# Sliding-window attention and a GeGLU block on one core: the first batch's opening run loaded in f32 by one queue, its row sums inverted on ScalarE, and two out tiles computed by halves

## The chip, the core and the metric

The kernel runs on one core of a Trainium2 chip. TensorE (PE in the profile) multiplies, VectorE (DVE) and ScalarE (ACT) work on its results, GpSimd (POOL) here clears memory and issues loads, SyncE (SP) issues transfers. All transfers share the core's 16 DMA engines. The metric is device time in microseconds of one execution; the kernel before took 346.55 us (median of three runs, 346.27 to 348.04).

## The reference

Attention with a window of 128 keys and a penalty that grows with distance, then a gated feed-forward block over all tokens. Inputs and the result are f32.

```python
# q, k, v: (8 batches, 8 heads, 576, 64)
scores = scale * np.matmul(q, k.transpose(0, 1, 3, 2))
rel = pos[:, None] - pos[None, :]
bias = slopes[:, None, None] * (-np.abs(rel))[None]
mask = (rel >= 0) & (rel < 128)
attn = softmax(np.where(mask, scores + bias, -1e9))
x = np.matmul(attn, v)                  # to (4608 tokens, 512)
g, val = x @ w_gate, x @ w_val          # 512 x 1536 each
out = (gelu(g) * val) @ w_out           # 1536 x 512
```

## The kernel before

A batch has 576 rows, a group of the feed-forward block 512 tokens, so that nine groups follow eight batches. The work of each engine stands in an order written out by hand (`manual_schedule`); what is emitted first for an engine is done first on it. PSUM has eight banks; `bank()` takes the one that came free longest ago. Attention of a batch is computed in between the out tiles of the group before it; only batch 0 has nothing ahead of it, and the change is there.

**Heads and pairs.** Two heads share 128 partitions: pair c holds heads 2c and 2c+1, and there are four pairs. Scores are computed with keys on the partitions, so that the probabilities `P` serve as the right operand for the values without a transpose; the sums over keys are matmuls with ones.

**Loading batch 0.** Its q and k come in two "runs" (`RUNS`): rows 0 to 383, three consecutive rows to a partition, and rows 384 to 575. Of the first run, heads 0 to 3 come as f32 by SP (q) and ScalarE (k), two heads a load, into `raw`, which borrows space of `wo`; `cast` makes bf16 of a pair (`pairs0`), and `first` transposes it, three matmuls for a pair, with `untangle` copying the result to `qT` or `kT`. Heads 4 to 7 come by POOL's queue, which casts on the way (`load_runs(0, 0, 4, 8)`, line 127), and `second` transposes them head by head (twelve matmuls a tensor). The second run also comes by POOL into `vb[1]`, is copied by VectorE to `pairs1` (line 728), and is transposed by `rest`. After these, POOL issues v of the batch (three tiles, then two), the gate and value weights in pieces of columns, batch 1's q and k, the last weights, both halves of w_out (line 774), and batch 1's v. A load on POOL's queue is issued only when the eighth one before it has landed.

**Scores of the first 384 rows.** `biases0` puts the distance penalty of a pair in two banks by a matmul with `slopes`, `scores0` adds the scores, and an exp on ScalarE of 128x512 a head writes `P` (line 193). Scores of the remaining rows come later (`scores0_rest`): they get their penalty by a multiplication with `emask` on VectorE (line 196). `emask` is made by `decays` on ScalarE, 192 columns a head, and its last columns by copies on VectorE (`masks_of_last_blocks`, line 672).

**Sums and values of the first 384 rows.** `sums4` collects the sums of all heads in 32-row parts of one bank with `ones8` (line 343), VectorE inverts them (line 348). `products_first` multiplies P with v in four banks, and ScalarE copies them to `recip` (line 490). `spread_first` spreads the inverses over 64 rows a head by sixteen f32 matmuls with `sel8` (line 357) and multiplies on VectorE into `xT` (line 518). For batches 1 and 2 the kernel has another way, in `values_and_sums`: sums in 64 rows a head with `ones64`, inverted on ScalarE as Exp(-Ln(x)) (lines 452 and 453), no spread. The last 192 rows of batch 0 have a third: `products_rest`, `inverse_rest` (reciprocals, line 509), `scale_rest`.

**Group 0.** `gate_val(g, f, lo, hi)` multiplies 128 columns of the gate and value weights with tokens lo to hi of xT; Gelu on ScalarE (line 545) and a product on VectorE (line 546) write `hT`. Block f=0 comes as two halves of 192 tokens, f=1 to 8 with 384 tokens, then f=0 to 8 with the other 128, then f=9 to 11 with all 512. Then come twelve matmuls for each of four out tiles (`out_part`, line 575, in quarters of three), with batch 1's scores, sums and values between; `todo[0]` holds the order. Functions of one table of ScalarE must be loaded before they are used; the first load in the head is for Exp, the second for Gelu.

**Two halves of a bank.** Where matmuls with key rows 0 to 63 and rows 64 to 127 add into one bank, `products` and `sums4` let a no-op of SP or VectorE stand between them (`relay`, line 318), which waits for the first half and releases the second.

Of the kernel before, what the change touches and what calls it, by code (L numbers as in the profile page):

```python
# [7 lines left out]
FP32 = mybir.dt.float32  # L8
# [13 lines left out]
COLUMNS0 = ((0, 192, 384), (None, None, 448, 640, 832))  # L22
# [5 lines left out]
def kernel(  # L28
# [32 lines left out]

    def bank():
        return psum.tile([128, 512], FP32, name="ps")
# [22 lines left out]
    sel0 = consts.tile([128, 8], FP32, name="sel0")  # L86
    sel8 = consts.tile([128, 4, 64], FP32, name="sel8")
# [147 lines left out]
    def scores0(cs, pss):  # L235
        for c, ps in zip(cs, pss):
            for n in range(3):
                for x in (0, 1):
                    q0 = 128 * n + 64 * x
                    w = min(192, 384 - q0)  # L240
                    for i in (0, 1):
                        score(0, c, i, 2 * n + x, q0, w,
                              ps[i][64 * x:64 * x + 64, 192 * n:192 * n + w], False)
        for c, ps in zip(cs, pss):
            for i in (0, 1):
                exp(prob(0)[:, c, i, 0:512], ps[i])


    def scores0_rest(cs, later):
        pss = []  # L250
        for c in cs:
            ps = [bank(), bank()]
            pss.append(ps)
            for n, skip, w, col in ((2, 64, 128, 0), (3, 0, 192, 128), (4, 0, 64, 320)):
                for x in (0, 1):
                    for i in (0, 1):
                        score(0, c, i, 2 * n + x, 128 * n + 64 * x + skip, w,
                              ps[i][64 * x:64 * x + 64, col:col + w])
        for c, ps in zip(cs, pss):
# [3 lines left out]
            later.append((dst, emask[:, 2 * c:2 * c + 2, 64:448]))  # L263
# [58 lines left out]
    def sums4(b, s, between=None, added=True):  # L322
        first, w = shape(b, s)
        ps = bank()
        mms = ([], [])
        for h in range(H):
            for x in (0, 1):
                t = first + w * x
                g, a = 2 * x + h // 4, 32 * (h % 4)
                if b and added:  # L330
                    mms[0].append((g, ones8[:, a:a + 32], T[:, h, t:t + w], 0, w))
                    continue
                for m, q0, q1, col in pieces(b, t, t + w):
                    half = slice(64 * (m % 2), 64 * (m % 2) + 64)
                    mms[m % 2].append((g, ones8[half, a:a + 32],
                                       Ps[b % 2][half, h, col:col + q1 - q0], q0 - t, q1 - t))
        for half in (0, 1):
            if half and mms[1]:
                by = relay(mm)
                if between:  # L340
                    between()
            for n, (g, lhsT, rhs, lo, hi) in enumerate(in_turn(mms[half]) if mms[half] else ()):
                mm = nc.tensor.matmul(  # L343
                    out=ps[32 * g:32 * g + 32, lo:hi], lhsT=lhsT, rhs=rhs,
                    start=half == 0 and n < 4, stop=True, skip_group_check=True)
                if half and n == 0:
                    depends(mm, by)
        nc.vector.reciprocal(row(b)[:, first:first + w], ps[:, 0:w])  # L348

    def spread4_banks(b, s):  # L350
        lo, w = shape(b, s)
        pss = [bank() for _ in range(4)]
        for n in (0, 1):

            rows = sel8[:, 2 * n:2 * n + 2, :].rearrange("p i m -> p (i m)")
            for g, ps in enumerate(pss):
                nc.tensor.matmul(  # L357
                    out=ps[:, w * n:w * n + w], lhsT=rows[32 * g:32 * g + 32, :],
                    rhs=row(b)[32 * g:32 * g + 32, lo:lo + w], start=True, stop=True,
                    tile_position=(32 * g, 0))  # L360
        return pss

    def spread4(b, s, copies):
        lo, w = shape(b, s)
        for g, ps in enumerate(spread4_banks(b, s)):
            c, x = 2 * (g % 2), g // 2
            copies[g](out=recip[b][:, c:c + 2, lo + w * x:lo + w * x + w],
                      in_=ps[:, 0:2 * w].rearrange("p (c x) -> p c x", c=2))
# [21 lines left out]
    def products(b, banks):  # L390
        pss = [bank() for _ in range(1 + max(u[0] for u in banks))]
        todo, mid = [], 0
        for x in (0, 1):
            at = 0
            for odd in (x, 1 - x):
                if odd != x:
                    mid = at = max(at, mid)
                wide, small = [], []
                for u, c, lo, hi, to in banks:
                    if u % 2 == odd:  # L400
                        (small if hi - lo == 64 else wide).extend(
                            (x, u, c, m, q0, q1, col, to, lo, hi)
                            for m, q0, q1, col in pieces(b, lo, hi) if m % 2 == x)

                ns, n = len(small), len(small) + len(wide)
                for k in range(n):
                    t = (small if (k + 1) * ns // n > k * ns // n else wide).pop(0)
                    todo.append((at, *t))
                    at += (t[5] - t[4]) * (1 if isinstance(t[2], int) else t[2].stop - t[2].start)
# [77 lines left out]
    def products_first(copies):  # L487
        n = PARTS[0][0][1]
        for c, ps in enumerate(products(0, [(c, c, 0, n, 0) for c in range(4)])):
            copies[c](out=recip[0][:, c, 0:n], in_=ps[:, 0:n])  # L490
# [22 lines left out]

    def spread_first():
        _, w = shape(0, 0)
        for g, ps in enumerate(spread4_banks(0, 0)):
            c, x = 2 * (g % 2), g // 2
            nc.vector.tensor_tensor(  # L518
                out=xT[:, c:c + 2, w * x:w * x + w], in0=recip[0][:, c:c + 2, w * x:w * x + w],
                in1=ps[:, 0:2 * w].rearrange("p (c x) -> p c x", c=2), op=ALU.mult)  # L520
# [67 lines left out]

    def out_last(g):
        for lo in (0, 256):  # L590
# [16 lines left out]
    raw = [wo[:, 3 + 3 * w:6 + 3 * w, :].rearrange("p a x -> p (a x)").bitcast(FP32)  # L607
           for w in (0, 1)]

    pairs0 = [t[0].rearrange("p j x -> p (j x)")[:, 0:768].rearrange(  # L610
        "p (x c y) -> p x c y", x=3, c=2) for t in (qs, ks)]
    pairs1 = wo[:, 9:12, :]
    for h in (0, 2):
        for w, src, queue in ((0, q, nc.sync), (1, k, nc.scalar)):
            queue.dma_start(
                out=raw[w].rearrange("p (h x) -> p h x", h=4)[:, h:h + 2, :],
# [4 lines left out]
    load_runs(0, 0, 4, 8)  # L621
# [10 lines left out]
    nc.gpsimd.memset(ones64, 1.0)  # L632
# [21 lines left out]
    def cast(w, c, copy):  # L654
        copy(out=pairs0[w][:, :, c, :].rearrange("p x (i d) -> p x i d", i=2),
             in_=raw[w].rearrange("p (c i x d) -> p c x i d", c=2, i=2, x=3)[:, c])

    made_slopes(0, 4)
    nc.vector.tensor_reduce(
        out=sel0, in_=ident.rearrange("p (g h r) -> p h g r", g=4, r=4)[:, :, :, 0],  # L660
        op=ALU.add, axis=mybir.AxisListType.X)

    load_w(512, 768)
    load_w(768, 1024)
    load_w(1024, 1280)
    for n in (0, 1):
        load_runs(1, n, 0, 8)
    load_w(1280, DFF)
# [15 lines left out]
    def rest(w, cs, copy):  # L684
        ps = bank().bitcast(BF16)
        p = 64 * w
        for n, c in enumerate(cs):
            for x in range(3):
                nc.tensor.transpose(
                    out=ps[:, 192 * n + 64 * x:192 * n + 64 * x + 64],  # L690
                    in_=pairs1[p:p + 64, x, 128 * c:128 * c + 128],
                    identity=ident[p:p + 64, p:p + 64])
        untangle(copy, 0, 1, w, cs[0], cs[-1] + 1, ps)

    def second(w, copies):
        ps = bank().bitcast(BF16)
        for c in (0, 1):
            transpose_runs(0, 0, w, 2 + c, ps[:, 384 * c:384 * c + 384])
        for c in (0, 1):
            untangle(copies[c], 0, 0, w, 2 + c, 3 + c, ps[:, 384 * c:384 * c + 384])  # L700

    held = [bank(), bank()]
    keep_busy(held[0], 10, 128)
    keep_busy(held[0], 44)
    decays(0, 2)
    cast(0, 0, dve)
    cast(1, 0, act)
    decays(2, 4)
# [5 lines left out]
    made_slopes(4, 8)  # L714
    ps0 = biases0((0,), 4)
    scores0((0,), ps0)
    held = [bank(), bank()]
    for w in (0, 1):
        first(w, 1, (dve, act)[w], held[w])
    second(0, (dve, dve))  # L720
    for t in kT + qT:
        nc.vector.memset(t[:, :, 576:640], 0.0)
    scores0((1,), biases0((1,)))
    second(1, (dve, dve))
    for c in (2, 3):
        scores0((c,), biases0((c,)))
    decays(5, 6)
    dve(out=pairs1.rearrange("p x (h d) -> p x h d", d=64),  # L728
        in_=vb[1].rearrange("p j x -> p (j x)")[:, 0:1536].rearrange(
            "p (h x d) -> p x h d", h=H, x=3))  # L730
    for cs in ((0, 1), (2, 3)):
        for w in (0, 1):
            rest(w, cs, dve)
    row(0)
    masks = []
# [5 lines left out]

    nc.scalar.copy(out=sel8, in_=sel0[:, 0:8:2].unsqueeze(2).to_broadcast((128, 4, 64)))
    sums4(0, 0, lambda: scores0_rest((0,), masks))
    products_first((act, act, act, act))
    masks_of_last_blocks(0, 4)
    for t in vb:
        nc.vector.memset(t[64:128, 4, :], 0.0)
    spread_first()
    decays(6, 8)
# [135 lines left out]
```

## Time and profile before

| what | us |
|---|---|
| median of three runs | 346.55 (346.27 to 348.04) |
| the profiled execution | 345.86 |
| its span, first to last instruction | 344.1 |
| PE busy | 333.4 (97%) |
| VectorE busy | 191.3 (56%) |
| ScalarE busy | 173.1 (50%) |
| first exp of scores starts | 6.74 |
| copy of the second run (line 728) starts | 11.04 |
| first gate matmul (line 539) starts | 18.29 |
| load of the Gelu table starts | 21.15 |
| gate of f=2 starts | 23.51 |
| first out tile (line 575) starts | 44.83 |

Times inside the execution count from the start of the span. A row of the profile names the line of the kernel, the engine, the operation, output and inputs, and the number of instructions; in square brackets stands the idle time of that engine just ahead of them, and what ended it. A matmul's end is modelled, so that the time from one start to the next says more about PE's pace than the length of one does. The granted clock of PE was 1.0 throughout.

### The profile page before, as it was taken

To read this page: it belongs to the slowest core of one execution; us is meant where nothing else is said; L and a number is where in the kernel's file an instruction comes from. 1 tells how busy PE (TensorE), PEld (TensorE's weight loads), DVE (VectorE), ACT (ScalarE), POOL (GpSimd) and SP (SyncE) were. 2 spreads that over 40 slices of the span, in tenths; PEclk is the share of its full clock that TensorE was granted. 3 is DMA by queue.
4 is the path that set the end of the run, shared out by engine and by line. 5 is a ranking of instruction groups with operands and counts; after the bars stand their busy time and mean duration, and the time that the engine had idled before them with its cause. 6 is when DMAs were issued, how large, how long until landed. Compare 5 with 4: busy or idle time off the path is not lost.

```text
span 344.1 us, 8080 instructions
## 1 busy us (share of the span) xinstructions
PE 333.4 (97%) x3299; PEld 171.0 (50%) x3338; DVE 191.3 (56%) x337; ACT 173.1 (50%) x334; POOL 107.6 (31%) x143
## 2 busy tenths in 40 slices
PE   8789999999999999999999999999999999999995
PEld 6566655444644454445444454445444544444443
DVE  6899564644589555944695369546774313303320
ACT  6674588537896338443753366344823133223322
POOL 9775763571193085008600680040000000000000
PEclk9999999999999999999999999999999999999999
DMA  9999999999699799989986999597115110020002
GB/s 171 171 196 190 206 168 120 146 170 186 133 142 175 149 155 183 200 156 111 183 176 130 113 181 183 94 141 102 63 34 107 61 65 0 0 93 30 0 32 91
DMA packets 149705, 43.09 MB, mean 125 GB/s; under 512 B 134532, under 2 KB 142628, under 8 KB 149668
## 3 DMA queue, kind: packets, MB, share of 16 engines
q0 software_dynamic: 108480, 18.49, 72.5%
q1 hardware_dynamic: 37744, 17.70, 22.1%
q10 hardware_dynamic: 3444, 6.38, 8.7%
q8 instruction: 26, 0.43, 0.5%
q14 instruction: 11, 0.09, 0.1%
HBM read 43.65 MB, written 9.53 MB: 155 GB/s over the span
## 4 chain that ended last, share of the span: by engine, by line
PE 91%; ACT 2%; DMA 2%; DVE 2%; issue 1%; POOL 1%; DVEq 0%; POOLq 0%; ACTq 0%
PE ps L539 53%; PE ps L575 27%; PE ps L425 5%; PE ps L188 2%; DMA vb<-in_k_dram 2%; PE ps L343 1%; ACT osb L580 1%; ACT P L193 1%; PE ps L593 1%; PE ps L144 1%; DVE xT L518 1%; DVE P L196 0%; ACT rb L452 0%; PE ps L357 0%; DVE wo L728 0%
## 5 line engine op out<-in xcount | busy, mean ns | idle before, releaser
L546 DVE TENSOR_TENSOR hT<-ps,gelu 128x512 bf16<-128x512 f32 (+3 forms) x118 | 74.3, 641 | 92.4 <-PE ps L539 80.3
L545 ACT ACTIVATE gelu<-ps 128x512 bf16<-128x512 f32 (+3 forms) x118 | 65.3, 561 | 103.3 <-PE ps L539 87.6
L539 PE MATMUL ps<-xT,wv 128*128 128x512 bf16 (+3 forms) x468 | 112.4, 361 | 0.4
L539 PE MATMUL ps<-xT,wg 128*128 128x512 bf16 (+3 forms) x457 | 111.2, 360 | 1.3 <-DVE xT L518 0.6
L575 PE MATMUL ps<-wo,hT 128*128 128x512 bf16 x402 | 94.4, 379 | 1.6 <-issue 0.6
L539 PEld LDWEIGHTS <-wv 128*128 128x128 bf16 x472 | 44.9, 98 | 48.8
L539 PEld LDWEIGHTS <-wg 128*128 128x128 bf16 x472 | 44.2, 98 | 48.7 <-issue 0.9
L193 ACT ACTIVATE P<-ps 128x384 bf16<-128x384 f32 (+2 forms) x128 | 56.1, 543 | 17.9 <-PE ps L188 17.7
L575 PEld LDWEIGHTS <-hT 128*128 128x128 bf16 x420 | 39.4, 98 | 46.7
L196 DVE TENSOR_TENSOR P<-P,emask 128x768 bf16<-128x768 bf16 (+1 forms) x60 | 34.5, 588 | 22.0 <-ACT P L193 21.1
L102 POOL DMA_DIRECT2D vb<-in_v_dram x40 | 33.8, 876 | 8.4 <-PE ps L188 2.2
L580 ACT COPY osb<-ps 128x512 f32<-128x512 f32 x29 | 17.4, 600 | 36.7 <-PE ps L575 36.5
L102 POOL DMA_DIRECT2D qs<-in_q_dram x30 | 25.2, 855 | 6.2 <-DMA wo<-in_moe_w_out_dram 4.4
L102 POOL DMA_DIRECT2D ks<-in_k_dram x30 | 25.4, 886 | 1.4 <-DMA qs<-in_q_dram 1.3
L836 POOL COPY mark<-hT 1x2 bf16<-1x2 bf16 x4 | 0.7, 176 | 78.6 <-DVE hT L546 78.6
L188 PE MATMUL ps<-qT,kT 64*64 64x192 bf16 (+2 forms) x656 | 19.3, 236 | 0.5 <-DVE kT L152 0.2
L188 PEld LDWEIGHTS <-kT 64*64 64x64 bf16 x656 | 13.0, 106 | 11.6 <-issue 8.1
L482 DVE TENSOR_TENSOR xT<-ps,rb 128x512 bf16<-128x512 f32 (+3 forms) x29 | 14.3, 564 | 6.4 <-PE ps L425 6.4
L425 PE MATMUL ps<-P,vb 64*64 64x192 bf16 (+2 forms) x736 | 17.5, 222 | 0.2
L425 PEld LDWEIGHTS <-vb 64*64 64x64 bf16 x736 | 14.6, 107 | 4.1 <-issue 2.7
L274 DVE TENSOR_TENSOR T<-P 64x1024 bf16<-64x1024 bf16 (+1 forms) x20 | 15.0, 751 | 0.4
L348 DVE RECIPROCAL r<-ps 128x128 f32<-128x128 f32 (+2 forms) x11 | 11.2, 1052 | 0.5 <-PE ps L343 0.5
(83 smaller groups left out, 156.5 us busy)
## 6 DMA issues: line engine op xcount, KB each, us to landing
out_dram<-osb SPq DMA_DIRECT2D x35, 256.0 KB
rb<-rd ACTq DMA_DIRECT2D x10, 576.0 KB
vb<-in_v_dram POOLq DMA_DIRECT2D x32, 128.0 KB, 6.4
qs<-in_q_dram POOLq DMA_DIRECT2D x24, 128.0 KB, 5.3
ks<-in_k_dram POOLq DMA_DIRECT2D x24, 128.0 KB, 6.3
wo<-in_moe_w_out_dram POOLq DMA_DIRECT2D x2, 768.0 KB, 14.7
wg<-in_moe_w_gate_dram POOLq DMA_DIRECT2D x5, 256.0 KB, 8.2
wv<-in_moe_w_val_dram POOLq DMA_DIRECT2D x5, 256.0 KB, 8.8
```

The costliest lines, as they stand in the source:

```text
L102: nc.gpsimd.dma_start(out=t[0:n, j, :].rearrange("p (h d) -> p h d", h=H), in_=src[b][:, 128 * j:128 * j + n, :].rearrange("h p d -> p h d"))
L188: nc.tensor.matmul(out=out, lhsT=keys(b, c, m)[half, :], rhs=qT[b % 2][half, c, q0:q0 + n], start=first, stop=True, skip_group_check=not f ...
L193: nc.scalar.activation(out=dst, in_=src, func=AF.Exp, scale=0.125)
L196: nc.vector.tensor_tensor(out=dst, in0=dst, in1=m, op=ALU.mult)
L274: nc.vector.tensor_tensor(out=to[half, :, 2 * n0 + x:2 * n1 + x - 1:2], in0=P[half, :, 3 * n0:3 * n1 - 2:3], in1=P[half, :, 3 * n0 + 1:3 * ...
L425: mm = nc.tensor.matmul(out=out, lhsT=lhsT, rhs=prob(b)[half, c, i, col:col + q1 - q0], start=all(t[2] != u for t in todo[:n]), stop=True, ...
L482: nc.vector.tensor_tensor(out=xT[:, c, at:at + e - a], in0=src, in1=recip[b][:, c, a:e], op=ALU.mult)
L539: nc.tensor.matmul(out=ps, lhsT=w[:, c, 128 * f:128 * (f + 1)], rhs=xT[:, c, t0 + lo:t0 + hi], start=begins, stop=(c == 3), skip_group_che ...
L545: nc.scalar.activation(out=gl[:, 0:n], in_=pg, func=AF.Gelu)
L546: nc.vector.tensor_tensor(out=hid[g][:, f, lo:hi], in0=pv, in1=gl[:, 0:n], op=ALU.mult)
L575: nc.tensor.matmul(out=acc[g], lhsT=hid[g][:, f, 128 * t:128 * (t + 1)], rhs=wo[:, f, :], start=(f == 0), stop=(f == NF - 1))
L580: (nc.vector.tensor_copy if g < B - 2 and t in by_dve.get(g, (0,)) else nc.scalar.copy)(out=osb, in_=acc[g])
```

## The change

All of it is in batch 0's head and group 0's first two out tiles.

- The first run of all eight heads comes uncast in f32, eight loads of two heads; SP issues seven of them, ScalarE the first of k. Heads 4 to 7 of raw data lie in batch 1's `qs` and `ks` tiles. `cast` and `first` now serve all four pairs, and `second` goes. POOL no longer issues `load_runs(0, 0, 4, 8)`; ahead of its first load it clears `ones64`, the last columns of kT and qT, and the last rows of both vb tiles (VectorE did most of this before).
- A pair's copies and casts are emitted between the two exps of the pair before, and around its scores.
- The sums of rows 0 to 383 are made per half of the heads (pairs 0 and 1, pairs 2 and 3) with `ones64`, 64 rows a head, in two banks of 192 tokens for two pairs each; ScalarE inverts each bank by Ln and Exp. The first half's come ahead of the second run's transposes. `sums4` for this part, `spread_first`, `products_first`, `sel0` and `sel8` go. The values come in banks laid out in the same way, and VectorE multiplies the bank with the inverse.
- Remaining scores: columns in another order, so that one mask of 192 columns serves twice. The copies of `masks_of_last_blocks` move behind block f=8 of the 384 tokens.
- Block f=1 comes in two halves of 192 tokens like f=0, and its Gelus come ahead of f=0's.
- The first two out tiles are computed by halves of six matmuls, both first halves ahead of the second ones.
- `products` was rewritten; the orders of its matmuls follow the same rule. The warm-up has 2 + 60 matmuls instead of 10 + 44.

```diff
-    for h in (0, 2):
-        for w, src, queue in ((0, q, nc.sync), (1, k, nc.scalar)):
-            queue.dma_start(
-                out=raw[w].rearrange("p (h x) -> p h x", h=4)[:, h:h + 2, :],
+    for h in (0, 2, 4, 6):
+        for w, src in ((0, q), (1, k)):
+            (nc.scalar if w and h == 0 else nc.sync).dma_start(
+                out=raw[w][h // 4].rearrange("p (h x) -> p h x", h=4)[:, h % 4:h % 4 + 2, :],
                 in_=src[0][h:h + 2, 0:384, :].rearrange("h (p r) d -> p h (r d)", r=3))
...
-    load_runs(0, 0, 4, 8)
+    nc.gpsimd.memset(ones64, 1.0)
+    for t in kT + qT:
+        nc.gpsimd.memset(t[:, :, 576:640], 0.0)
+    for t in vb:
+        nc.gpsimd.memset(t[64:128, 4, :], 0.0)
     load_runs(0, 1, 0, 8)
...
+    n0 = PARTS[0][0][1] // 2
+    def sums_first(c, u=0):
+        return [(u + x, slice(c, c + 2), n0 * x, n0 * x + n0, 0) for x in (0, 1)]
+    def values_first(c, u=0):
+        return [(u + x, c + i, n0 * x, n0 * x + n0, n0 * i) for x in (0, 1) for i in (0, 1)]
+    def inverse_first(c, x, ps):
+        to = recip[0][:, c:c + 2, n0 * x:n0 * x + n0]
+        src = ps[:, 0:2 * n0].rearrange("p (c x) -> p c x", c=2)
+        return (lambda: nc.scalar.activation(out=to, in_=src, func=AF.Ln),
+                lambda: nc.scalar.activation(out=to, in_=to, func=AF.Exp, scale=-1.0))
+    def scale_first(c, x, ps):
+        nc.vector.tensor_tensor(
+            out=xT[:, c:c + 2, n0 * x:n0 * x + n0], in0=ps[:, 0:2 * n0].rearrange("p (c x) -> p c x", c=2),
+            in1=recip[0][:, c:c + 2, n0 * x:n0 * x + n0], op=ALU.mult)
...
+    def out_half(g, t, part):
+        store()
+        if part == 0:
+            acc[g, t] = bank()
+        for f in range(6 * part, 6 * part + 6):
+            nc.tensor.matmul(
+                out=acc[g, t], lhsT=hid[g][:, f, 128 * t:128 * (t + 1)],
+                rhs=wo[:, f, :], start=(f == 0), stop=(f == NF - 1))
+        if part:
+            osb = o_pool.tile([128, DM], FP32, name="osb")
+            (nc.vector.tensor_copy if t == 0 else nc.scalar.copy)(out=osb, in_=acc[g, t])
...
+    cast(0, 2, dve)
+    cast(1, 2, dve)
+    scores0((0,), biases0((0,), 4), lambda: pair(1, (dve, act)))
+    cast(1, 3, act)
+    biases = biases0((1,))
+    pair(2, (dve, dve), lambda: cast(0, 3, dve))
+    scores0((1,), biases)
+    biases = biases0((2,))
+    pair(3, (dve, dve))
+    scores0((2,), biases)
+    scores0((3,), biases0((3,)))
+    row(0)
+    sums_a = products(0, sums_first(0))
+    for step in zip(*(inverse_first(0, x, sums_a[x]) for x in (0, 1))):
+        for do in step:
+            do()
+    dve(out=pairs1...)
...
-    sums4(0, 0, lambda: scores0_rest((0,), masks))
-    products_first((act, act, act, act))
-    masks_of_last_blocks(0, 4)
-    for t in vb:
-        nc.vector.memset(t[64:128, 4, :], 0.0)
-    spread_first()
-    decays(6, 8)
+    rest((dve, dve))
+    sums_b = products(0, sums_first(2))
+    for x in (0, 1):
+        ln, minus = inverse_first(2, x, sums_b[x])
+        ln()
+        decays(5 + x, 6 + x)
+        minus()
+    decays(7, 8)
+    vals = products(0, values_first(0) + values_first(2, 2))
+    for x in (0, 1):
+        for c in (0, 2):
+            scale_first(c, x, vals[c + x])
+    scores0_rest((0,), masks)
+    gate_val(0, 0, 0, n0, waiting)
     scores0_rest((1,), masks)
+    gate_val(0, 0, n0, 2 * n0, waiting)
...
-    gate_val(0, 1, 0, 384, waiting)
+    gate_val(0, 1, 0, n0, waiting)
+    gate_val(0, 1, n0, 2 * n0, waiting)
+    waiting = waiting[2:] + waiting[:2]
...
+    masks_of_last_blocks(0, 8)
     for f in range(9):
         gate_val(0, f, 384, 512)
...
-        0: [("table",), ("s", 1, 0, (0, 1)), 4, ("s", 1, 0, (2, 3)), 2, ("s", 1, 1, (0, 1)), 2, ("s", 1, 1, (2, 3), masks), ...],
+        0: [("table",), ("s", 1, 0, (0, 1)), ("o", 0, 0, 0), ("o", 0, 1, 0), ("s", 1, 0, (2, 3)), ("o", 0, 0, 1), ("s", 1, 1, (0, 1)), ("o", 0, 1, 1), ("s", 1, 1, (2, 3), masks), ...],
```

## The prediction

> **What bounds the kernel now.** I read the page's shares first, then who PE waited for after 30 us, then the chain of waits over the first 24 us, then ScalarE's and POOL's timelines there.
>
> The page, and PE's waits from 30 us to the end:
>
> ```profile
> span 344.1 us, 8080 instructions
> PE 333.4 (97%) x3299; PEld 171.0 (50%) x3338; DVE 191.3 (56%) x337; ACT 173.1 (50%) x334; POOL 107.6 (31%) x143
> ...
> PE ps L575 <- issue: 0.6, 4, 0.2
> ```
>
> After 30 us PE waits 0.6 us in all. Whatever PE does not lose ahead of its dense part is time off the end, one for one, as long as nothing later has to wait for data. The place to judge is the head. The chain of waits there (start, length, what):
>
> ```profile
> 1.35 0.90 POOL qs L127
> 2.25 0.75 POOL ks L127
> 3.00 0.67 POOL vb L127
> 3.67 7.27 DMA vb<-in_k_dram
> 10.94 0.03 issue
> ...
> 11.04 0.96 DVE wo L728
> ...
> 14.88 0.96 PE ps L425 x32
> ...
> 15.86 0.49 ACT rb L490
> ...
> 17.59 1.95 DVE xT L518 x4
> ...
> 22.29 1.28 PE ps L425 x47
> ```
>
> The chain starts with POOL issuing the loads of heads 4 to 7 (L127 qs, ks), then hangs on the second run's load (7.27 us), the copy of it, sums, copies to ScalarE, spread, scaling (1.95), masks, and the last products. The first 384-wide gate of block f=2 starts at 23.51 us (timeline). That is my mark: from it on, the two programs have the same PE work.
>
> ScalarE between 8 and 24 us:
>
> ```profile
> 10.49 2.06 ACT L193 ACTIVATE P<-ps 128x512 bf16<-128x512 f32 x4 [0.54 <-PE ps L188]
> 12.42 0.38 ACT L646 ACTIVATE emask<-wo 128x192 bf16<-128x192 bf16 x1
> ...
> 13.86 0.87 ACT L193 ACTIVATE P<-ps 128x384 bf16<-128x384 f32 x2 [0.76 <-PE ps L188]
> 15.86 1.63 ACT L490 COPY rb<-ps 128x384 f32<-128x384 f32 x4 [1.13 <-PE ps L425]
> ...
> 19.49 1.64 ACT L193 ACTIVATE P<-ps 128x384 bf16<-128x384 f32 x4 [0.73 <-PE ps L188]
> 21.15 1.28 ACT L545 ACT_TABLE_LOAD   x1
> ```
>
> Four idle gaps (0.54 to 1.13 us), and the table for Gelu loads only after the last exp of the head: no hT before 22.4. The last mark is a transfer; POOL's timeline gives the issue of the second half of w_out, the DMA view over its issue the time to landing:
>
> ```profile
> 29.62 0.82 POOL L774 DMA_DIRECT2D wo<-in_moe_w_out_dram  x1 [0.37 <-PE ps L539]
> wo<-in_moe_w_out_dram POOLq DMA_DIRECT2D x1, 768.0 KB, 16.0
> ```
>
> It lands at 45.6. The first out tile starts at 44.83; its seventh matmul, at 0.22 us each, needs that half at 46.15: only 0.55 us of slack.
>
> **The change, part by part.** I lay the new order along each engine: an instruction starts when the one ahead of it is over and its inputs are there, with spacings from the trace (exp 128x512 0.49 us, 128x384 0.375, exp of a mask row 0.265, DVE copy of a transpose 0.475, cast 0.335 on DVE and 0.41 on ScalarE, scale or mask 0.465).
>
> *Loads.* POOL loses two issues (0.90 + 0.75) and gains seven memsets. Its 128x64 memset took 0.17, its 64x512 0.52; 128x256 I put between, at 0.28: 0.17 + 4 x 0.28 + 2 x 0.52 = 2.3. So the second run is issued some 0.6 us later (3.6 for 2.98), and all behind it in POOL's queue: v, the weights. SP issues seven loads where it had two (0.45 each, done by 4.2; its relays are wanted only from 11 us on, so that is free); ScalarE issues one less. The four new loads are 256 packets of 768 B at 36 ns over 16 engines, 0.58 us each; by the landing records the first four landed at 3.85, 4.19, 4.96 and 5.33, so the rest land at about 5.9, 6.5, 7.1, 7.7. The two loads on POOL's queue that go were 1024 packets at about 460 per us, 2.2 us: equal transfer time. But the old stream reached the end of q and k only at 8.44; now it does so at about 7.7, and the stream behind it (v, weights, w_out: DMA near saturated until 50 us) comes 0.3 to 1.0 us earlier, less if POOL's later issue leaves a hole. v's third tile landed at 14.3; I take 13.6, bounds 13.0 and 14.9.
>
> *Casts and a rule.* DVE gets three casts of f32 in SBUF (0.43 each) between 5.9 and 8.9, while POOL issues. The Trainium skill (SBUF — State Buffer, Who interferes with whom) says a copy or cast on VectorE in a two-port mode shuts GpSimd out of a shared port for the whole instruction, so the descriptors of a POOL-issued DMA are written late. In the trace the three v issues took 0.89, 0.89, 0.90 us, the second under such a cast (5.43 to 5.84): not lengthened. By the row nothing; by the rule v comes up to 1.3 us later, which would cost 1 us of the end (rival 1). I take the row.
>
> *Scores.* PE's warm-up is 2 x 0.107 + 60 x 0.053 = 3.41 us, as before. Pair 0 is unchanged (scores 6.27, exp 6.74). DVE then has the casts of pair 2 ahead of pair 1's copy: 5.9, 6.5, free at 6.85, and the copy was due at 6.99: hidden by 0.15 us. ScalarE takes pair 1's copy between the two exps: that pair's scores at 8.2 (8.41 before). Pairs 2 and 3 follow at 9.65 and 10.5; the last exp ends at 12.2 (12.56).
>
> *Sums on ScalarE.* Out go the sums with 32-row columns (0.63 + 1.07 on PE), a reciprocal (1.36), the copies to recip (1.63), the spread (16 f32 matmuls, 0.93) and sel's upkeep. In come 32 matmuls with ones (0.6 us per half of heads, by the 128-to-384-wide ones at 22.3), four Ln and four Exp. The nearest rows are the 128x512 ones of batch 1: 0.58 to 0.63; for 384 columns about 0.5, spaced 0.38 and 0.42. First half's sums 10.9 to 11.5: they need neither the second run nor v. Its transposes then fill PE while the last exps run (12.1), sums of the second half 12.9. ScalarE: two Ln and two Exp 12.1 to 13.7, the other four with three mask rows between to 16.1. v at 13.6 opens the values; 64 matmuls end at 14.9 (48 took 1.21). DVE scales at 14.65, 15.1, 15.6 and, after the last Exp at 15.9, 16.05 to 16.6: done there where it was 19.54.
>
> *To the mark.* Gate f=0 at 15.2 to 17.1 between the remaining scores; their exps run at 16.1, 16.9, 17.6 and 18.4 per pair, ending at 19.3. Table load to 20.6; Gelu and product of f=1 free two PSUM banks at 21.3. The masks end at 19.9, products of the rest 19.9 to 21.2. So f=2 starts at **21.3**, against 23.51: **2.2 us**. With v at 14.9 it is 22.2 (1.3); v earlier than 13.3 gains 0.3 more, then ScalarE's order sets it.
>
> *After it.* The mask copies (0.70 + 0.71 on DVE) move behind f=8, 1.0 to 1.6 us together, ahead of the products of the 128-wide gates; PE is four blocks of 0.45 us ahead by its banks, so 0 to 0.5 is lost, 0.15 taken. The reciprocals keep DVE full; scale_rest then ends 0.7 us before PE wants it (0.9 before). Weights landed 3.0 to 3.9 us before use; 2.2 earlier is covered.
>
> *Out tiles by halves.* The same 24 matmuls. Without it, the second half of w_out would be wanted at 46.15 - 2.2 = 43.95, 1.6 before it lands. Now twelve matmuls and a group of scores (0.45) go ahead of its first use: 6 x 0.22 + 0.45 = 1.8 later, at 45.7 against 45.6 or earlier. Cost nothing by that cover; two accumulators hold two banks 1.3 us longer, with exps done in time.
>
> Sum: 2.2 - 0.15 = 2.05. Against the profiled execution (345.86 = 344.1 of span and 1.8 around it) 343.8; against the median shown, 346.55, which is 0.7 above it, **344.5**; I say **344.4**, since one of its three runs was high.
>
> **Rivals.** (1) v or the second run comes late (port lock, a hole behind POOL's memsets, a slower shared queue). For it: v is wanted at 12.9, a wait that the old order did not have. Against: equal transfer time. Gain 1.1: 345.4.
> (2) The change is hidden: the streams saturate the DMA engines, so w_out or a weight comes when it came, plus 0.6 for POOL's delay, and PE waits; most is given back. 346.0. Against: 3 us of slack, and halves.
> (3) Better: the stream comes 1 us earlier and the masks cost nothing: 343.3.
> (4) Slower: SP's single queue. ScalarE holds the cast of the last k (due 8.1) ahead of six exps; if it lands at L, they end at L + 3.4 for 12.1, and the mark moves by L - 8.7. It decides from L = 10.75 on, when the queue needs 1.16 us for each of the five loads after 4.96; at 1.5 us L is 12.5, the mark 25.1: 348.2. For it: queue order, and POOL's packets share the engines from 6.4. Against: SP's queue moved 162 packets in half a us beside ScalarE's 90, 0.8 us a load even shared.
>
> **How the numbers follow.** Main case 0.60, (1) 0.15, (2) 0.07, (3) 0.12, (4) 0.06. A measurement tells about 0.5% (1.7 us) from no change. Faster: main and (3), 0.72; same: (1) and (2), 0.22; slower: 0.06. Main case alone 343.7 to 345.0; the range takes in (3), (1) and most of (2): 343.1 to 346.1.
>
> **What would show it.** Right: first half's sums on PE before the second run's copy on DVE; Ln and Exp without gaps on ScalarE from 12 to 16; the Gelu table at 19.3; f=2 at 21.3; no PE wait ahead of the out tiles. Wrong: PE waiting for v past 14.3; ScalarE or DVE waiting for qs or ks past 8; a PE wait in the 128-wide gates over 0.5; a wait at the seventh or thirteenth matmul of the out tiles.

## The result, and the profile after

The changed kernel takes 344.97 us (median; 344.58 to 345.20) beside 346.85 us for the kernel before on the same chip: a ratio of 0.994, 95% interval 0.991 to 0.997. In a later set of runs it was 344.89 beside 345.51, a ratio of 0.9983 (0.9964 to 1.0003). So the gain is 1.9 us in the first set (four executions of each kernel) and 0.6 us in the later one (22 and 51), whose interval includes no change; the spans of the profiled executions put it at 1.0 to 1.3 us (343.1 and 342.8 for 344.1). The forecast was 344.4, a gain of 2.05. In the later set 17 executions of the changed kernel took 343.93 to 345.54 us at a mean granted clock of PE of 0.999 or 1.0, and the other five 346.34 to 347.81 at 0.988 to 0.995.

The page of the kernel after, and PE's waits after 30 us:

```profile
span 342.8 us, 8041 instructions
PE 332.3 (97%) x3272; PEld 170.7 (50%) x3310; DVE 190.9 (56%) x331; ACT 174.4 (51%) x339; POOL 108.3 (32%) x147
```

```profile
PE ps L550 <- issue: 0.5, 3, 0.2
PE ps L392 <- SPq L320: 0.2, 1, 0.2
PE ps L570 <- issue: 0.2, 1, 0.2
```

PE is as dense as before once the head is over. The mark of the prediction, the start of f=2's gate, is at 22.14 us (23.51 before, 21.3 predicted). From the mark to the end of the span it is 320.66 us (320.59 before): all that was won and lost lies ahead of the mark. The chain of waits of the kernel after in that stretch (start, length, what):

```profile
3.81 5.80 DMA ks<-in_k_dram
...
9.64 0.51 ACT ks L650
10.15 2.93 ACT P L192 x6
13.08 0.77 ACT rb L467 x2
13.85 0.82 ACT rb L468 x2
...
17.00 3.05 ACT P L192 x8
...
20.07 1.28 ACT L520
...
21.73 0.37 DVE hT L521
...
22.14 1.95 PE ps L514 x11
```

The second run, its copy, the spread and the scaling, which held the chain before, are gone from it. In their place stands one load: the last k (heads 6 and 7), issued last of SP's seven, landing at 9.61. From there ScalarE has no gap up to the table for Gelu. ScalarE around that load, from its timeline:

```profile
7.89 0.60 ACT L192 ACTIVATE P<-ps 128x512 bf16<-128x512 f32 x1
9.64 0.51 ACT L650 CAST ks<-ks 128x384 bf16<-128x384 f32 x1 [1.15 <-DMA ks<-in_k_dram]
10.05 3.03 ACT L192 ACTIVATE P<-ps 128x512 bf16<-128x512 f32 x6
```

It stood idle for 1.15 us with six exps queued behind that cast, pair 1's two among them, whose scores on PE were done at 8.7. The last exp of the 384 rows ends at 13.08; it was 12.56 before and 12.2 in the prediction.

A second thing was late, at the very start. VectorE's and POOL's timelines after:

```profile
1.30 1.07 DVE L629 TENSOR_SCALAR ident<-tmpl 128x128 bf16<-128x128 f32 x1
1.40 1.58 DVE L631 TENSOR_SCALAR far<-tmpl 128x128 f32<-128x128 f32 x2
```

```profile
1.22 0.56 POOL L615 MEMSET kT<- 128x256 bf16 x2
1.73 0.56 POOL L615 MEMSET qT<- 128x256 bf16 x2
2.34 1.10 POOL L617 MEMSET vb<- 64x512 bf16 x2
3.40 0.82 POOL L126 DMA_DIRECT2D vb<-in_q_dram  x1
```

The same two lines of VectorE before:

```profile
1.29 0.19 DVE L634 TENSOR_SCALAR ident<-tmpl 128x128 bf16<-128x128 f32 x1
1.40 0.36 DVE L636 TENSOR_SCALAR far<-tmpl 128x128 f32<-128x128 f32 x2
```

While POOL clears, VectorE's identity takes 1.07 us for 0.19, and what VectorE does next follows 0.9 to 1.2 us later: its first cast starts at 4.77 for 3.87.

So there are two candidates for the 0.85 us by which the mark missed 21.3. **Theory A**: the landing of the last k. Each later event is tied to it through ScalarE's queue. **Theory B**: VectorE's late start behind POOL's clearing.

### The profile page after: what moved, and what is told of

The parts are those of the page before. It is cut to its first block, busy times and chain, and to the rows that moved or that the text cites. A ratio compares the mean times of both kernels' runs of the same rounds, so it can differ in the third digit from the quotient of the medians.

```text
span 342.8 us, 8041 instructions
## 1 busy us (share of the span) xinstructions
PE 332.3 (97%) x3272; PEld 170.7 (50%) x3310; DVE 190.9 (56%) x331; ACT 174.4 (51%) x339; POOL 108.3 (32%) x147
## 4 chain that ended last, share of the span: by engine, by line
PE 89%; ACT 6%; DMA 2%; issue 1%; SPq 1%; DVE 0%; ACTq 0%
PE ps L514 54%; PE ps L550 25%; PE ps L392 4%; ACT P L192 3%; PE ps L187 2%; DMA ks<-in_k_dram 2%; PE ps L570 2%; PE ps L334 1%; ACT osb L555 1%; SPq L607 1%; PE ps L584 1%; PE ps L143 1%; ACT rb L468 0%; ACT rb L467 0%; ACT L520 0%
## 5 line engine op out<-in xcount | busy, mean ns | idle before, releaser
L550 PE MATMUL ps<-wo,hT 128*128 128x512 bf16 x380 | 89.0, 379 | 1.4 <-issue 0.5
L550 PEld LDWEIGHTS <-hT 128*128 128x128 bf16 x396 | 37.2, 98 | 44.3
L392 PE MATMUL ps<-P,vb 64*64 64x64 bf16 (+2 forms) x752 | 17.8, 220 | 0.3 <-SPq L320 0.2
L425 DVE TENSOR_TENSOR xT<-ps,rb 128x512 bf16<-128x512 f32 (+1 forms) x10 | 6.4, 639 | 6.8 <-ACT rb L420 6.7
```

The costliest lines, as they stand in the source:

```text
L392: mm = nc.tensor.matmul(out=out, lhsT=lhsT, rhs=prob(b)[half, c, i, col:col + q1 - q0], start=all(t[2] != u for t in todo[:n]), stop=True, ...
L550: nc.tensor.matmul(out=acc[g], lhsT=hid[g][:, f, 128 * t:128 * (t + 1)], rhs=wo[:, f, :], start=(f == 0), stop=(f == NF - 1))
```

## The experiments

Where a kernel is timed, the ratio is to the kernel before on the same chip, with its 95% interval. "Mark" is always the start of f=2's gate. A time is a median over all executions; marks, landings and spans are those of the one execution that was traced. Unless said otherwise an edit is to the changed kernel and leaves the computation as it is.

### 1. The last k by ScalarE's queue

```diff
-            (nc.scalar if w and h == 0 else nc.sync).dma_start(
+            (nc.scalar if w and h in (0, 6) else nc.sync).dma_start(
```

> One edit to the changed kernel: the last load of k (heads 6 and 7) is issued by ScalarE, behind its first one, and not as the last of SP's seven. Theory A (the last k's landing at 9.61 us holds ScalarE's queue, and so sets the mark, the start of f=2's gate): k lands at 5.5 to 6.5, ScalarE casts it without a wait, the last exp ends at 12.3 to 12.5 for 13.08, the mark moves from 22.14 to 21.3 to 21.6, and the time falls by 0.5 to 0.8 us against the changed kernel. Theory B (VectorE's late start, 4.84 for 3.67 us, behind POOL's clearing sets it): the first scores stay at 6.44 and the mark at 22.0 to 22.2; the time stays.

Measured: 344.0 us, ratio 0.9956 (0.9944 to 0.9968). ScalarE's timeline:

```profile
8.29 0.61 ACT L192 ACTIVATE P<-ps 128x512 bf16<-128x512 f32 x1
8.78 0.52 ACT L650 CAST ks<-ks 128x384 bf16<-128x384 f32 x1
9.18 3.23 ACT L192 ACTIVATE P<-ps 128x512 bf16<-128x512 f32 x6
```

No wait for k; the last exp ends at 12.42, the mark is at 21.47, the span 342.2. That is A's number. The scatter goes too: 21 of its 22 executions lie between 343.98 and 344.09 us, where those of the changed kernel run from 343.93 to 347.81. So the edit takes away late executions, and the fastest ones are no faster. But B is not out: with the load gone from the chain of waits, this stands at its front instead:

```profile
1.38 0.99 DVE ident L629
2.37 0.62 DVE far L631 x2
...
4.85 0.34 DVE qs L650
...
5.24 0.82 PE ps L665 x6
```

A sets the mark in the changed kernel, and by this chain B stands right behind it.

### 2. POOL clears later, its loads start earlier

```diff
-    for t in kT + qT: ...memset...
-    for t in vb: ...memset...
     load_runs(0, 1, 0, 8)
     load_v(0, (0, 1, 2))
+    for t in kT + qT: ...memset...
+    for t in vb: ...memset...
```

> One edit to the changed kernel: POOL clears the columns of kT and qT and the rows of vb only behind its issues of the second run and of v, so that its loads start about 1.7 us earlier and VectorE starts without it. Theory B (VectorE's late start sets the mark): identity in 0.2 us for 1.07, slopes at 3.7, first scores at 6.27, mark at 21.0 to 21.9. Theory A (the last k's landing sets it): POOL's packets share the engines with SP's queue from about 4.5 us on, the last k lands later than 9.61, at 10 to 10.6, and the mark is at its landing plus 12.5, 22.5 to 23.1; the time rises by 0.4 to 1.0 us although v and the second run come over 1 us earlier.

Measured: 348.6 us, ratio 1.0082 (1.0056 to 1.0109): slower than the kernel before. VectorE's identity is back at 0.19 us, so B's cause is gone, and yet the mark is at 26.12. ScalarE:

```profile
8.49 0.51 ACT L650 CAST ks<-wo 128x384 bf16<-128x384 f32 x1 [2.25 <-DMA wo<-in_k_dram]
...
12.54 0.51 ACT L650 CAST ks<-ks 128x384 bf16<-128x384 f32 x1 [1.92 <-DMA ks<-in_k_dram]
```

POOL's packets flow from 3.9 us on instead of 6.1, and SP's queue beside them moves 68 to 146 packets in half a us where it moved 182 to 256 without them. The second k lands at 8.47 for 5.49, the last at 12.52 for 9.61. The direction is A's; the size was far off in my expectation (22.5 to 23.1), since I let only the last two loads suffer.

A second thing adds to it, which my expectation didn't have: PE's granted clock. The pages give it in 40 slices of some 8.6 us, as tenths of full speed (9 is 90% or more); the changed kernel, then this run:

```profile
PEclk9999999999999999999999999999999999999999
PEclk9699999999999999999999999999999999999999
```

In finer windows the clock is 0.50 here from 9.0 to 15.8 us, after PE had stood idle for 1.77 us, up to 9.06, waiting for the cast of the second k. Two bias matmuls take 1.04 us there for 0.60, and ScalarE now waits for PE between the exps:

```profile
14.46 1.08 ACT L192 ACTIVATE P<-ps 128x512 bf16<-128x512 f32 x2 [0.43 <-PE ps L187]
15.98 1.09 ACT L192 ACTIVATE P<-ps 128x512 bf16<-128x512 f32 x2 [0.43 <-PE ps L187]
```

The chain of waits runs over the third k (landed at 10.65) and PE's work at that clock. Ten of the 12 executions have a mean clock of 0.989 or 0.990; the one at 0.999 took 346.43 us.

This is rival (4) of the prediction in the flesh, with its own case worked out there: landing at 12.5, mark at 25.1, 348.2 us. The run gave 12.52, 26.12 and 348.6. The landing alone, with 3.47 us to the last exp and 9.06 from there to the mark as in the other traces below, would have made 25.05 (an estimate; no traced run has such a landing at the full clock). It leaves 1.07 us for the clock, which the rival didn't have.

### 3. POOL held until the first q is there, VectorE clears in its gaps

```diff
+    nc.gpsimd.tensor_copy(out=mark, in_=raw[0][0][0:1, 0:1].bitcast(BF16))
-    for t in kT + qT: nc.gpsimd.memset(...)      # now VectorE, behind the copy of the second run
-    for t in vb: nc.gpsimd.memset(...)           # now VectorE, ahead of its first scaling
```

> The changed kernel with the clearing given to VectorE in later gaps, and POOL held by a two-element copy until the first q is there, so that its loads start at about 4.0 us, a little later than the 3.40 of the changed kernel. Theory A: the last k lands at 8.9 to 9.4 since POOL's packets come later, the mark is at its landing plus 12.5, 21.4 to 21.9. Theory B: VectorE's start is free again (identity 0.2 us), first scores at 6.27, and the mark moves by that 0.2 to 1.2 us whatever the last k does; if k lands at 9.6 as before and the mark is still under 22.0, B has a share.

Measured: 344.53 us, ratio 0.9959 (0.9943 to 0.9976), span 341.9. POOL issues its first load at 4.28 (3.40), its packets come 0.6 to 0.8 us later, and SP's seven loads are all but through before them: the last k lands at 8.05. ScalarE:

```profile
8.08 0.51 ACT L647 CAST ks<-ks 128x384 bf16<-128x384 f32 x1 [0.30 <-DMA ks<-in_k_dram]
8.49 3.28 ACT L192 ACTIVATE P<-ps 128x512 bf16<-128x512 f32 x6
```

The last exp ends at 11.77, and the mark is at 21.25, which is what the prediction had for the change itself (21.3). The chain now begins with the loads that were held:

```profile
7.58 5.88 DMA vb<-in_v_dram
...
13.51 0.96 PE ps L392 x42
...
21.25 2.76 PE ps L514 x16
```

With A and B both gone, v's third tile sets the mark. This run alone doesn't part A from B, since both are removed in it. Beside experiment 1, A alone is worth 22.14 - 21.47 = 0.67 us at the mark, and B on top 0.22 before v cuts it off (its exps end 0.65 earlier). But the traced execution (343.66 us) is the fastest of 22, 0.9 under their median, and that median lies above experiment 1's 344.0: that B's removal shortens the time is not shown.

### 4. Only the loads, and all but the loads

All but the loads: the sums on ScalarE, the masks and the out tiles of the change, with the loads, casts and clearing of the kernel before.

```diff
-    for h in (0, 2, 4, 6):
-        for w, src in ((0, q), (1, k)):
-            (nc.scalar if w and h == 0 else nc.sync).dma_start(
+    for h in (0, 2):
+        for w, src, queue in ((0, q, nc.sync), (1, k, nc.scalar)):
+            queue.dma_start(
...
-    nc.gpsimd.memset(...)
+    load_runs(0, 0, 4, 8)
```

> The part with the sums on ScalarE, the masks and the out tiles by halves, but with the loads, casts and clearing of the kernel before (heads 4 to 7 of the first run cast on POOL's queue). Theory A: the new loads cost more than they bring, since the last exp ends at 13.08 with them and at 12.56 without; here it ends at 12.5 to 12.7, v lands at 14.3, the mark is at 21.6 to 21.9, and the time is 0.2 to 0.5 us under the changed kernel. Rival (the early v and second run are what gains): v 0.66 later carries the mark to 22.7 or later, and the time is 0.5 us or more above the changed kernel.

Measured: 344.54 us, ratio 0.9963 (0.9942 to 0.9985), span 341.9, mark 21.41, last exp at 12.36. ScalarE needs no uncast k of heads 6 and 7 here:

```profile
8.78 1.08 ACT L192 ACTIVATE P<-ps 128x512 bf16<-128x512 f32 x2 [0.51 <-PE ps L187]
10.29 2.07 ACT L192 ACTIVATE P<-ps 128x512 bf16<-128x512 f32 x4 [0.43 <-PE ps L187]
```

Only the loads: the kernel before, with the new loads and casts.

> The kernel before with the new loads alone: all heads of the first run uncast by SP and ScalarE, casts on VectorE and ScalarE, POOL clearing ahead of its loads; sums, spread, masks and out tiles as before. Theory A (the loads bring the last k late): the last exp of the 384 rows ends at about 13.1 for 12.56 of before, the mark at 23.4 to 24.0 for 23.51, time 0 to 0.5 us above before. Rival (what the loads do for v and the second run, both 0.6 us earlier, is what counts): mark at 22.8 to 23.1, 0.4 to 0.7 us under before.

Measured: 371.37 us, ratio 1.0749. My edit left batch 1's loads of q and k where the kernel before issues them, ahead of the casts. The raw data of heads 4 to 7 lies in those same tiles, so the casts waited for batch 1's rows and took those; that part of the computation is changed in this run, and it doesn't bear on A. PE's waits:

```profile
PE ps L686 <- DVE qs L661: 23.0, 2, 22.2
```

What it shows is that the tiles lent to the raw data make the order of issue binding: the change moves the later weights and batch 1's loads behind the casts because it has to. With them moved:

```diff
-    load_w(512, 768) ... load_runs(1, n, 0, 8) ... load_w(1280, DFF)
     ...
     dve(out=pairs1...)
+    load_w(512, 768) ... load_runs(1, n, 0, 8) ... load_w(1280, DFF)
```

> The kernel before with the new loads and casts, as in the run with the new loads and the old sums, but the later weights and batch 1's q and k are issued where the changed kernel issues them, behind the casts that read the same tiles (in that run they stood ahead, so the casts of heads 4 to 7 waited for batch 1's rows and read those). Theory A (the loads bring the last k late): last exp of the 384 rows ends at about 13.1 for 12.56, mark at 23.4 to 24.0 for 23.51, time within 0.5 us of before or above. Rival (v and the second run 0.6 us earlier are what counts): mark at 22.8 to 23.1, time 0.4 to 0.7 us under before.

Measured: 346.0 us beside 345.95, ratio 1.0 (0.9985 to 1.0016), span 344.0, mark 23.70, last exp at 13.71. The number is the one that A gave, but the chain of waits doesn't run over the last k here (landed at 9.62, its cast at 9.64 without a wait); it starts with VectorE:

```profile
1.38 0.99 DVE ident L640
...
4.96 0.34 DVE qs L661
```

So in that order of work the chain has B in front. The four kernels together, by the mark: neither part 23.51, loads alone 23.70, the rest alone 21.41, both 22.14 (22.41 the second time). **By these traces the rest is worth 2.1 us; the loads cost 0.2 without it and 0.7 to 1.0 with it.** The medians, each against the kernel before on its chip, say less: loads alone the same, the rest alone 1.1 us faster, both 0.6 faster. The gain of the rest stands (ratio at most 0.9985). No run shows that the loads, as the change has them, bring anything; that they cost 0.4 us is not shown, since the intervals of the last two overlap (0.9942 to 0.9985 and 0.9964 to 1.0003).

### 5. The first two out tiles whole

```diff
-        0: [("table",), ("s", 1, 0, (0, 1)), ("o", 0, 0, 0), ("o", 0, 1, 0), ("s", 1, 0, (2, 3)), ("o", 0, 0, 1), ("s", 1, 1, (0, 1)), ("o", 0, 1, 1), ...
+        0: [("table",), ("s", 1, 0, (0, 1)), 4, ("s", 1, 0, (2, 3)), 2, ("s", 1, 1, (0, 1)), 2, ...
```

> One edit to the changed kernel: group 0's first two out tiles are computed whole, in quarters of three matmuls as before, not by halves. Theory (halves cover the second half of w_out, which lands at 45.62): the mark stays at 22.1; that half is wanted at 46.15 - 1.37 = 44.8, PE waits 0.6 to 0.9 us at the seventh matmul of the first out tile, and the time is 0.6 to 0.9 us above the changed kernel. Rival (the halves are worth nothing, since something else spaces the out tiles): no PE wait over 0.2, same time.

Measured: 345.9 us, ratio 1.0007 (0.9989 to 1.0024), on the chip where the changed kernel itself was 344.89; the two intervals just overlap (0.9964 to 1.0003 there), and the wait itself is in the trace. PE's waits after 30 us:

```profile
PE ps L550 <- DMA wo<-in_moe_w_out_dram: 0.9, 1, 0.9
```

The mark was at 22.85 (its last k landed at 10.33, in the same head as the changed kernel's), and from mark to end 321.75 us for 320.69: 1.06 us are the out tiles'. The second half of w_out landed at 46.42 here, 0.8 later than in the changed kernel's trace, so part of the wait is this execution's own. The half was wanted at 45.55; with the changed kernel's mark, 0.71 earlier, and its landing at 45.62 the wait would have been 0.8 (an estimate). In the changed kernel it landed at 45.62, and the second halves start at 46.52 by PE's timeline: 0.9 us of slack.

### 6. Both causes away

```diff
-            (nc.scalar if w and h == 0 else nc.sync).dma_start(
+            (nc.scalar if w and h in (0, 6) else nc.sync).dma_start(
...
+    nc.gpsimd.tensor_copy(out=mark[:, 0:1], in_=slopes[0:1, 0, 0:1])   # then POOL's loads
...                                                  # clearing by VectorE as in experiment 3
```

> Both causes taken away in the changed kernel: the last k issued by ScalarE, the clearing given to VectorE in later gaps, and POOL held until VectorE has made the first slopes (about 3.5 us), so that its loads are issued as early as in the changed kernel. Theory (A and B one behind the other, then v): last k landed before 6.5, last exp ends by 11.8, v at 13.1 to 13.3, mark at 20.8 to 21.2, time 0.9 to 1.4 us under the changed kernel. Rival (with A gone nothing else counts): the mark is at 21.4 to 21.5, as with the last k by ScalarE alone.

Measured: 344.62 us, ratio 0.9973 (0.9961 to 0.9984), span 342.8, mark 22.06: neither my number nor the rival's. Two things went another way. ScalarE's second load goes ahead of SP's others, so that these land one place later (the second k at 6.02 for 5.49); the last exp ends at 12.59, not 11.8. And v's third tile landed at 14.02, with my own clearing of vb behind it in the chain:

```profile
6.88 7.13 DMA vb<-in_v_dram
...
14.06 0.96 PE ps L392 x42
...
15.07 0.22 DVE vb L747
...
15.38 0.57 DVE xT L471
```

With that clearing moved behind the one of kT and qT, and nothing else changed:

> The kernel with both causes taken away, but VectorE clears the last rows of vb right behind the columns of kT and qT, not ahead of its first scaling, where it took 0.3 us of the chain. Theory (the mark follows v's third tile by 7.7 us once the exps are early): with v at 14.0, as in that run, the mark is at 21.7 to 21.8; with v at 13.2, 20.9 to 21.1; time 0.3 us under that run or more. Rival (ScalarE's order sets the mark, not v): the mark stays at 22.0 to 22.1.

Measured: 344.2 us, ratio 0.9948 (0.9928 to 0.9967), span 342.5, mark 21.63, v at 13.48. This is 0.4 us under the run above (on another chip), but by neither account of mine. The chain runs over loads, casts and exps:

```profile
2.78 4.48 DMA ks<-in_k_dram
...
10.50 2.08 ACT P L192 x4
12.58 0.77 ACT rb L467 x2
...
21.63 3.41 PE ps L514 x20
```

### 7. The changed kernel again

> The changed kernel itself, so that the other three can be set beside it on one chip: mark at 22.1, last k at 9.6, ratio to before 0.994 to 0.998.

Measured: 344.89 us, ratio 0.9983 (0.9964 to 1.0003), span 343.1, mark 22.41, last k at 9.88.

### One rule for all of them

In the kernels with the new sums, the mark is the later of two things: the end of the last exp of the 384 rows plus 9.06 us (ScalarE's four Ln, four Exp, three masks, eight exps, table and Gelu, then VectorE's hT), and the landing of v's third tile plus 7.78. The first constant is the changed kernel's 22.14 - 13.08, the second experiment 3's 21.25 - 13.47.

| kernel | last k lands | last exp + 9.06 | v + 7.78 | mark | span |
|---|---|---|---|---|---|
| changed | 9.61 | (22.14) | 21.38 | 22.14 | 342.8 |
| changed, again | 9.88 | 22.42 | 21.40 | 22.41 | 343.1 |
| 5, whole tiles | 10.33 | 22.85 | 21.47 | 22.85 | 344.6 |
| 1, k by ScalarE | early | 21.48 | 20.93 | 21.47 | 342.2 |
| 2, POOL earlier | 12.52 | 26.13 | 22.24 | 26.12 | 346.8 |
| 3, POOL held | 8.05 | 20.83 | (21.25) | 21.25 | 341.9 |
| 4, old loads | none | 21.42 | 20.64 | 21.41 | 341.9 |
| 6, first | early | 21.65 | 21.80, and 0.3 of clearing | 22.06 | 342.8 |
| 6, second | early | 21.64 | 21.26 | 21.63 | 342.5 |

The two values in brackets give the constants; the later of the two columns meets the mark of every other row within 0.04 us. The last k's landing enters where it holds back ScalarE: 9.61 to 13.08 is 3.47 (3.4 in the prediction's rival), 9.88 to 13.36 and 10.33 to 13.79 the same to 0.02. In experiment 2 it is 4.55, since the exps of the later pairs wait for PE at its lower clock. The rule is about the traced executions: it says nothing of how often a load lands late.

## Why the prediction was right in sign and short in size

**The time.** 344.97 lies in the stated range, but that range reaches 346.1, above what the kernel before itself took in the three later sets (medians 345.51 to 345.95). That the gain of the first set, 1.88, comes near the forecast 2.05 is luck: the kernel before was high in it (346.27 to 348.04).

**What bounds the kernel.** Right. What PE didn't lose ahead of the mark came off the end one for one: mark to end is 320.5 to 320.9 us in all traces but experiment 5's (321.75), the loads alone (320.3) and the 371 us run of experiment 4.

**Loads: the step that failed.** "So the rest land at about 5.9, 6.5, 7.1, 7.7" took the pace of SP's queue with the engines to itself. They landed at 6.15, 7.06, 7.79 and 9.61. The pace held up to 6.1 us; then POOL's first packets came and SP's queue fell from 182 to 256 packets in half a us to 82 to 96, beside some 110 of POOL's. "At 0.8 us a load even shared", said against rival (4), came from SP beside ScalarE's queue, not beside POOL's; the last load took 1.8. The price that the rival put on it was right: 21.3 + (9.61 - 8.7) = 22.2, measured 22.14. The main case needed that formula with its own landing time, not a threshold of 10.75 for being slower than before. By experiment 1, whose exps end at 12.42 without a wait for k, a landing costs from about 12.42 - 3.47 = 8.95 on. One of the prediction's own signs of being wrong, ScalarE waiting for ks past 8, came true.

**POOL's clearing.** The sum counted it on POOL alone (2.3 us; first load at 3.6, measured 3.40). Its other side, VectorE blocked, was left out. It put the first scores at 6.44 for 6.27, and with A gone it stands at the front of the chain. B was no part of the measured miss while A held; removing both brought 21.25, in the fastest of 22 executions.

**The rule on the shared port.** I weighed only one direction of it: VectorE's casts against POOL's issues. There the row was right on POOL's side, three v issues in 2.70 us after, 0.90 each, as before. The Trainium skill (SBUF — State Buffer, Who interferes with whom) says that when VectorE is in a two-port mode, whichever of the two issues first keeps the shared ports for its whole instruction and the other one waits; the cost then falls on VectorE when POOL is first, and the runs agree: 1.07 us for 0.19 behind the clearing, until four clearings in a row are over (at 2.29). Three of the five casts that VectorE makes while POOL issues took 0.65 to 0.69 us, the other two 0.40 and 0.41; both casts before took 0.41 to 0.43, beside POOL's issues too. So what lengthened the three is not shown.

**v and the stream.** v's third tile at 13.60, predicted 13.6: right, but with luck in it. The 0.3 to 1.0 us that the stream was to gain did not come (second half of w_out at 45.62, before 45.59), and in experiment 4 the old loads brought v at 12.86, in the order of issue that gave 14.26 before. One execution's tail of a load is no base for a step of half a us.

**Sums on ScalarE.** Right: first half's sums ahead of the second run's transposes, Ln and Exp spaced 0.38 and 0.41, no gap from there on. But with the last k late these sums came at 11.58, behind the second run's copy (11.06), not ahead of it as the prediction's sign had it. This part, with the masks and the out tiles, is worth 2.1 us at the mark in the traces and 1.1 by the medians (experiment 4), where the main case had 2.2 for the whole.

**Mask copies behind f=8.** 0.15 put down, nothing found: no PE wait in the 128-wide gates, 320.66 for 320.59 from mark to end.

**Out tiles by halves.** Right: no wait with them, 0.9 us without.

**Sum.** 2.2 at the mark became 1.37; less nothing for the masks, for 0.15. The span fell by 1.3.

## What to carry to other kernels

When a change puts several loads on one hardware queue, time the last one with the other queues' packets flowing, and look who stands behind its consumer: a cast ahead of six exps made a load that came 1.9 us late cost 0.7 us at the mark (experiment 1). Split a change into its halves before believing in both: here the loads, as the change had them, brought nothing that any run shows, and the rest brought the gain. Compare medians as well as traces: the traced execution of experiment 3 was the fastest of 22. Moving the last urgent load to a second queue made nearly all executions alike, 1.6 us under the kernel before; with the bulk stream started earlier, the loads came so late that PE stood idle, its clock was at half for 6.8 us, and the kernel was slower than before the change.

## What the runs showed that I had not expected

- **Clearing on POOL stalls VectorE.** VectorE's tensor_scalar from SBUF to SBUF took 1.07 us for 0.19 behind POOL's memset in the changed kernel and in experiments 1 and 5, and 0.19 in 2, 3, 6 and with the old loads in 4, where POOL doesn't clear then. The two instructions behind it took 1.58 for 0.36.
- **SP's queue beside POOL's loses more than half of its pace**: 93 packets of 768 B in half a us beside 110 of 384 B, where alone it moved 182 to 256.
- **One of sixteen engines decides when a load is there.** In the first run of experiment 6, fifteen engines had finished v's third tile by 12.21 us and the last by 14.02; the first v tile 10.48 and 12.57. A single packet of instructions, 16 KB, took 0.97 us at 10.45 in that run. Whether it lay on the late engine the records don't say, since they don't name engines. A like packet of 0.96 to 1.30 us stands between 9.4 and 11.7 us in every trace, and in the changed kernel it starts at 11.36, behind the last k, so that it can't have made that load late.
- **The changed kernel scatters more than its sums say**: the last k landed at 9.61, 9.88 and 10.33 in three executions with the same head, and the mark followed each time.
